# Moving splits, sums and raw weight loads in the last stage of an attention, expert and gated-layer kernel

## The chip, the cores and the metric

The kernel runs on one core of a Trainium2 chip. The metric is the device time of one launch in microseconds, as the median of several runs. Below, PE is the matrix engine (TensorE), DVE is VectorE, ACT is ScalarE, POOL is GpSimd and SP is SyncE, which here only issues DMAs.

## The reference

Three parts follow each other. The change is in the third; its core is quoted, the first two are told.

1. Attention without softmax: for each of 8 x 8 heads, `kv = k^T v`, `out = q kv`, then a root-mean-square norm of each row. This gives 4608 tokens of width 512.
2. A mixture of 8 experts: each token goes to the expert of its largest logit, through `relu(x w1) w2`, and is weighted by its softmax probability.
3. A gated layer over all 4608 tokens, width 512 to 1536 to 512:

```python
gate = 1.0 / (1.0 + np.exp(-(x @ w_gate)))
val = x @ w_val
return (gate * val @ w_out).astype(np.float32)
```

## The kernel before

The third part starts about 630 us into the span and is cut into 60 steps, 0 to 59. Tokens come in five blocks, `b` = 0 to 4 (`NB`); each block has 12 steps (`NJ`), one for each 128 of the 1536 inner columns. Step `s` is column slice `j = s % 12` of block `s // 12`. In blocks 1 to 4 a step holds two halves of 512 tokens.

Numbers are carried as pairs: each operand is split by ACT into a rounded high part (a copy) and by DVE into the low part (a subtraction), and each product is three matmuls, high by high, high by low, low by high. A split is therefore one ACT instruction followed by one DVE instruction.

**The gated unit.** `glu_unit` (matmuls in lines 1010 to 1012) computes gate and value of a step by Strassen's scheme in Winograd's form: seven products, numbered 1, 6, 7, 5, 2, 4, 3 in that order, of six 128x512 matmuls each. They go to the `gv` banks of PSUM, of which four rotate. DVE sums them (line 1014), ACT applies two sigmoids (1034, 1043), and DVE multiplies (1044, 1045) into two tiles `g` of the step.

**Spots.** Between the products the unit calls `at(p)`, and `prepare(s, p)` then issues other work. `SPOTS = (0, 1, 6, 7, 5, 2, 4, 3)` is their order in time: spot 0 before product 1, spot 1 after it, 6 after product 6, and so on, 3 at the step's end. Each engine executes what is issued to it in the order of issue, so the order in which `prepare` calls its parts is the order of each queue. This order is written out by hand.

**Inputs of the next block (Y).** During the last steps of a block the next block's rows are loaded (`load_y`), weighted (`weigh_y`), transposed on PE into a `gv` bank and copied to `yraw` by ACT (`flip_y`, line 1284), then summed (`sum_y`, line 1257) and split (`split_y`, ACT 1252, DVE 1253) into the seven right-hand operands. `YPLAN` gives the step and spot of each letter; splits and sums there are 1024 columns wide.

**Output products.** Blocks 0 and 1 multiply `g` by `w_out` plainly (`out_step`, lines 1380 to 1382, operands from `ready_o` and `load_o`). From block 2 (`FIRST` = 24) the output also goes by Strassen, in chunks. A chunk `(b, n, m)` is one of seven products `n` for one of six pairs `m` of column slices: 12 matmuls of 128x256 in `run_chunk` (lines 1480 to 1482). `place_chunks` puts products 1 and 7 of pair `m` into step 6 + m of the block itself, and products 2, 4, 6, 5, 3 into the first five steps after it, six chunks a step. For the last block these stand alone after step 59, at the end of the program. `ready_chunk` forms and splits a chunk's left operand (ACT 1453, DVE 1446; for n = 7 one more DVE subtraction first, for n = 2 one more after), `load_chunk` fetches its weights three chunks ahead, `sum_g` combines two pairs of `g` tiles by two DVE instructions (1463, 1464), and `combine` takes a finished product out of PSUM. `gh` and `gl`, the split operands, have three buffers each. `chunk_step` calls all of these at each spot from step 30 (`OPEN`); it stands last in `prepare`, behind the Y work.

**Combined output weights.** In steps 24 to 29 `sums_o` loads two raw rows of `w_out` (DMA, line 1398), subtracts quarters of them (four DVE instructions, 1403), splits both (ACT 1407, DVE 1408) and stores them (`wp_d`, 1409).

Of the kernel before, what the change touches and what calls it, by code (L numbers as in the profile page):

```python
# [25 lines left out]
NB = 5  # L26
# [58 lines left out]
def attention_moe_glu_kernel(  # L85
# [271 lines left out]
    with ExitStack() as st:  # L357
# [342 lines left out]
        for b in range(B):  # L700
# [6 lines left out]
            for r in range(5):  # L707
# [22 lines left out]
                early = b == B - 2  # L730
# [135 lines left out]
        for n in range(NFRONT * NJ1 + 1):  # L866
            t, j = divmod(n, NJ1)
# [343 lines left out]
    with ExitStack() as st:  # L1211
# [4 lines left out]
        NJ = F2 // 128  # L1216
# [106 lines left out]
        def new_wos():  # L1323
            return xp.tile([128, 2, DM], F32R, tag=wos_tags.pop(), name="wos")
# [43 lines left out]
        def out_step(*steps):  # L1368
            work = []
            for sz in steps:  # L1370
                if sz in step_at:
                    b, h, k = step_at[sz]
                    if k == 0:
                        acc[b, h] = [pac.tile([128, DM], F32, tag=f"ac{i}", name=f"ac{i}") for i in range(HT)]
                    work.append((b, h, k, split_o.pop(sz), *split_g.pop(sz)))
            for i in range(HT):
                for b, h, k, wos, gh, gl in work:
                    o, cs = acc[b, h][i], slice(i * 128, i * 128 + 128)
                    wh, wl = wos[:, 0], wos[:, 1]
                    nc.tensor.matmul(out=o, lhsT=gh[:, cs], rhs=wh, start=(k == 0), stop=False)  # L1380
                    nc.tensor.matmul(out=o, lhsT=gh[:, cs], rhs=wl, start=False, stop=False)  # L1381
                    nc.tensor.matmul(out=o, lhsT=gl[:, cs], rhs=wh, start=False, stop=(k == NJ - 1))  # L1382
                    if k == NJ - 1:
                        store_out(b, h, i, len(work) > 1)
# [3 lines left out]
        def sums_o(s, spot):  # L1388


            m = s - FIRST
            if not 0 <= m < NJ // 2:
                return
            if spot == 0:
                for i, pool in enumerate((y0p, late_pool[0])):
                    k = 2 * m + i
                    wo_raw[i] = pool.tile([128, DM], F32, tag="wo", name="wo", bufs=1)
                    nc.sync.dma_start(out=wo_raw[i], in_=w_d[k // 4][:, k % 4, 1024:1536])
            if spot == 5:
                b11, b12 = (wo_raw[0][:, n * 256:n * 256 + 256] for n in range(2))  # L1400
                b21, b22 = (wo_raw[1][:, n * 256:n * 256 + 256] for n in range(2))
                for o, x, y in ((b11, b12, b11), (b12, b22, b12), (b22, b22, b11), (b21, b21, b22)):
                    nc.vector.tensor_tensor(out=o, in0=x, in1=y, op=ALU.subtract)
            if spot in (2, 3):
                i = int(spot == 3)
                src, t = wo_raw[i], new_wos()
                nc.scalar.activation(out=t[:, 0], in_=src, func=ACTF.Copy)
                nc.vector.tensor_tensor(out=t[:, 1], in0=src, in1=t[:, 0], op=ALU.subtract)
                nc.sync.dma_start(out=wp_d[2 * m + i][:, :, :], in_=t.bitcast(F32))
# [6 lines left out]
        chunks, chunk_pos, chunks_ready, chunk_at, sum_at = [], [], [], {}, {}  # L1416

        def place_chunks(b):

            s0 = NJ * b  # L1420
            early = [(6, 5, 4), (7, 5, 4), (8, 5, 4), (9, 5, 4), (10, 5, 4), (11, 5, 4)]
            if b == NPLAIN:
                early[0:3] = [(7, 6, 5), (7, 2, 4), (8, 5, 4)]
            for m, (j, *spots) in enumerate(early):
                for spot, n in zip(spots, (1, 7)):
                    chunk_at.setdefault((s0 + j, spot), []).append((b, n, m))
                sum_at.setdefault((s0 + max(j + 1, 2 * m + 2), 1), []).append((b, m))
            seq = [(b, n, m) for m in range(6) for n in (2, 4)] + [(b, n, m) for n in (6, 5, 3) for m in range(6)]
            for i, c in enumerate(seq):
                chunk_at.setdefault((s0 + NJ + i // 6, SPOTS[1 + i % 6]), []).append(c)  # L1430

        def load_chunk(q):
            if q < len(chunks):
                b, n, m = chunks[q]
                src, odd, half = OPERAND[n]
                nc.sync.dma_start(out=b_slots[q % 4].bitcast(F32), in_=src[2 * m + odd][:, :, half * 256:half * 256 + 256])

        def ready_chunk(q):


            if q >= len(chunks):
                return
            b, n, m = chunks[q]
            g = G[b]
            a11, a12, a21, a22 = (2 * m, 0), (2 * m + 1, 0), (2 * m, 1), (2 * m + 1, 1)
            sub = lambda o, x, y: nc.vector.tensor_tensor(out=o, in0=x, in1=y, op=ALU.subtract)  # L1446
            if n == 7:
                src = free_g.pop(0)
                sub(src, g[a11], g[a21])
            else:  # L1450
                src = g[{1: a11, 2: a12, 4: a22, 6: a11, 5: a21, 3: a12}[n]]
            hi, lo = (ws.tile([128, HC], F32R, tag=t, name=t, bufs=3) for t in ("gh", "gl"))
            nc.scalar.activation(out=hi, in_=src, func=ACTF.Copy)  # L1453
            sub(lo, src, hi)
            split_c[q] = (hi, lo)
            if n == 2:
                sub(g[a12], g[a12], g[a11])
            elif n != 1:
                free_g.append(src)

        def sum_g(b, m):
            g = G[b]
            nc.vector.tensor_tensor(out=g[2 * m, 1], in0=g[2 * m, 1], in1=g[2 * m + 1, 1], op=ALU.add)
            nc.vector.tensor_tensor(out=g[2 * m, 0], in0=g[2 * m, 1], in1=g[2 * m, 0], op=ALU.subtract)
# [66 lines left out]
        b_slots, later_o = [], []  # L1531
# [20 lines left out]
                load_chunk(q)  # L1552

        def chunk_step(s, spot):
            for b, m in sum_at.get((s, spot), ()):
                sum_g(b, m)
            now = 8 * s + SPOTS.index(spot)
            if later_o:
                later_o.pop(0)()
            if now in chunk_pos:  # L1560
                q = chunk_pos.index(now)
                run_chunk(q)
                load_chunk(q + 3)
            q = len(chunks_ready)
            while q < len(chunks) and chunk_pos[q] <= now + 3 and (q < 2 or chunk_pos[q - 2] <= now):
                chunks_ready.append(q)
                ready_chunk(q)
                q += 1

        yr = {}  # L1570

# [65 lines left out]
        def prepare(s, spot):  # L1637


            b, j = divmod(s, NJ)  # L1640
            if spot == 0:
                load_wt(s + 1)
                if s + 2 <= NJ:
                    load_raw(s + 2, s + 1)
                load_rows(s + 2)
                decode_late(s)
                sum_w(s + 1)
            if spot == 6:
                ready_o(s, 1)
                load_o(s + 1, 0)  # L1650
                load_o(s + 1, 1)
            if spot == 1:
                group(s + 1, 0)
            if spot == 7:
                out_step((s, 0))
            if spot == 2:
                group(s + 1, 1)
            if spot == 4:
                ready_o(s + 1, 0)
                out_step((s, 1))  # L1660
            if b + 1 < NB:
                for what, do in TURNS[min(b, 1)].get((j, spot), ()):
                    what(b + 1, do)
                if s == 9 and spot == 0:
                    hold_y(mw[1].tile([128, 2, 2, 2, HC], F32R, tag="w2r1", name="w2r1"))
                if s == 11 and spot == 3:
                    hold_y(yA[0][:, 0:2])
                if b and j == NJ - 1 and spot:
                    free_y.append(Y.pop((b, spot)))
                for what in YPLAN[min(b, 1)].get((j, spot), ""):  # L1670
                    y_step(b + 1, what)
            if b > 1:
                for what in YPLAN[1].get((j + NJ, spot), ""):
                    y_step(b, what)
            if spot == 3:
                decode_late2(s)
            sums_o(s, spot)
            if (s, spot) == (FIRST, 0):
                yslots.extend(xp.tile([128, XW], F32, tag="xg", name="yr", bufs=4) for _ in range(2))
                free_g.extend(xp.tile([128, XW], F32, tag="xg", name="yr", bufs=4)[:, 0:HC] for _ in range(2))  # L1680
            if (s, spot) == (OPEN, 3):
                open_chunks()
            chunk_step(s, spot)

        bank = lambda n: pgv.tile([128, 512], F32, tag="gv", name="gv")
        tmp = lambda n: ws.tile([128, HC], F32, tag=n, name=n, bufs=1)
# [11 lines left out]
        OPEN = FIRST + 6  # L1698
# [43 lines left out]
```

## Time and profile before

| | |
|---|---|
| median of 3 runs | 1504.77 us (1502.82 to 1508.97) |
| the profiled execution | 1506.11 us, its span 1504.0 us |
| PE matmul / weight load busy | 1430.7 us (95%) / 1241.8 us (83%) |
| DVE, ACT, POOL busy | 1008.2 us (67%), 675.0 us (45%), 254.3 us (17%) |
| mean granted PE clock | 0.990 |
| HBM traffic | 250 GB/s over the span |

Busy is the time in which an engine executes; a waiting instruction is idle time. A clock of 1.00 is full speed. The shares are means over stages that differ, so the stretches that the change touches are read one by one below.

### The profile page before, as it was taken

How to read it: one execution, taken by the hardware profiler on the slowest of the kernel's cores; microseconds unless marked ns; L12 is line 12 of the kernel's file. 1: busy time of each engine (PE TensorE's matmuls, PEld its weight loads, DVE VectorE, ACT ScalarE, POOL GpSimd, SP SyncE). 2: the span in 40 equal slices, each digit the busy share in tenths (PEclk: the TensorE clock that was granted, in tenths of full speed). 3: DMA queues.
4: the chain of work that ended last, by engine and by line, in shares of the span. 5: the costliest groups of instructions: out<-in, count | busy, mean ns of one | idle time of the engine just before them, and what ended most of it. 6: DMA issues, size and time to landing. Idle time of an engine off the chain costs nothing.

```text
span 1504.0 us, 24818 instructions
## 1 busy us (share of the span) xinstructions
PE 1430.7 (95%) x9302; PEld 1241.8 (83%) x9302; DVE 1008.2 (67%) x1594; ACT 675.0 (45%) x1080; POOL 254.3 (17%) x350
## 2 busy tenths in 40 slices
PE   6988999999999999999999999999899999999995
PEld 6887789999999997778888777788788887998885
DVE  1667868888888886568766665456755567555663
ACT  3666455556556557555433332232433324322242
POOL 1021122322212222020111001020023200131014
PEclk9999999999999999999999999999999999999998
DMA  9977598998986758499976557785466654565544
GB/s 306 342 261 260 173 355 286 283 309 291 289 291 189 256 197 277 156 359 331 352 253 250 203 209 279 283 294 184 153 211 225 223 182 154 196 214 200 187 124 129
DMA packets 189707, 365.33 MB, mean 243 GB/s; under 512 B 22544, under 2 KB 114448, under 8 KB 182416
## 3 DMA queue, kind: packets, MB, share of 16 engines
q1 hardware_dynamic: 177408, 330.37, 65.0%
q0 software_dynamic: 10816, 32.08, 5.9%
q8 instruction: 75, 1.23, 0.3%
q10 hardware_dynamic: 1360, 1.26, 0.2%
q14 instruction: 48, 0.39, 0.1%
HBM read 301.31 MB, written 74.93 MB: 250 GB/s over the span
## 4 chain that ended last, share of the span: by engine, by line
PE 44%; DVE 6%; DMA 3%; ACT 2%; issue 1%; SPq 1%; POOL 0%; another core or an unknown queue 0%; POOLq 0%; DVEq 0%; ACTq 0%
PE gv L1010 8%; PE gv L1011 8%; PE gv L1012 8%; PE ac L1482 4%; PE ac L1480 3%; PE ac L1481 3%; DMA wo<-w_d 2%; PE ac L1380 2%; PE ac L1381 2%; PE ac L1382 2%; DVE u L1014 1%; PE gv L986 1%; PE gv L984 1%; PE gv L985 1%; PE tr L947 1%
## 5 line engine op out<-in xcount | busy, mean ns | idle before, releaser
L279 PE MATMUL ph<-xh,w1h 128*128 128x256 f32 x576 | 168.4, 292 | 5.6 <-ACT xh L261 4.6
L280 PE MATMUL ph<-xh,w1l 128*128 128x256 f32 x576 | 164.8, 286 | 0.9 <-DVE w1l L237 0.9
L281 PE MATMUL ph<-xl,w1h 128*128 128x256 f32 x576 | 164.9, 286 | 0.0
L1014 DVE TENSOR_TENSOR u<-u,gv 128x512 f32<-128x512 f32 x144 | 98.5, 684 | 95.9 <-PE gv L1012 90.8
L1482 PE MATMUL ac<-wos,gl 128*128 128x256 f32 x504 | 145.0, 288 | 9.8 <-DVE gl L1446 9.4
L1480 PE MATMUL ac<-wos,gh 128*128 128x256 f32 x504 | 144.0, 286 | 5.5 <-ACT gh L1453 5.3
L1481 PE MATMUL ac<-wos,gh 128*128 128x256 f32 x504 | 142.6, 283 | 0.0
L1011 PE MATMUL gv<-half,wt 128*128 128x512 f32 x336 | 131.7, 392 | 0.7 <-DVE half L1253 0.7
L1010 PE MATMUL gv<-half,wt 128*128 128x512 f32 x336 | 132.0, 393 | 0.0
L1012 PE MATMUL gv<-half,wt 128*128 128x512 f32 x336 | 130.9, 389 | 0.0
L279 PEld LDWEIGHTS ph<-xh,w1h 128*128 128x128 f32 x576 | 112.1, 195 | 8.0 <-ACT xh L261 4.8
L280 PEld LDWEIGHTS ph<-xh,w1l 128*128 128x128 f32 x576 | 112.2, 195 | 2.8 <-DVE w1l L237 1.1
L281 PEld LDWEIGHTS ph<-xl,w1h 128*128 128x128 f32 x576 | 112.0, 194 | 0.3 <-DVE xl L263 0.3
L1482 PEld LDWEIGHTS ac<-wos,gl 128*128 128x128 f32 x504 | 96.2, 191 | 14.1 <-DVE gl L1446 13.4
L336 PE MATMUL py<-w2l,hh 128*128 128x512 f32 x272 | 106.8, 393 | 0.1
L335 PE MATMUL py<-w2h,hh 128*128 128x512 f32 x272 | 106.7, 392 | 0.0
L337 PE MATMUL py<-w2h,hl 128*128 128x512 f32 x272 | 106.1, 390 | 0.0
L1480 PEld LDWEIGHTS ac<-wos,gh 128*128 128x128 f32 x504 | 96.2, 191 | 11.9 <-ACT gh L1453 7.6
L1043 ACT ACTIVATE u<-u 128x512 f32<-128x512 f32 x48 | 30.4, 633 | 153.0 <-DVE u L1014 150.7
L1481 PEld LDWEIGHTS ac<-wos,gh 128*128 128x128 f32 x504 | 96.3, 191 | 3.1
L1490 POOL DMA_INDIRECT out_dram<-ot,to x48 | 52.8, 1101 | 272.0 <-ACT ot L1512 180.4
L349 POOL DMA_INDIRECT y_d<-y,sidx x36 | 40.9, 1135 | 286.0 <-ACT y L345 96.5
(370 smaller groups left out, 3668.4 us busy)
## 6 DMA issues: line engine op xcount, KB each, us to landing
wt<-wt_d SPq DMA_DIRECT2D x36, 1536.0 KB
half<-in_moe_w_dram SPq DMA_DIRECT2D x96, 512.0 KB
w1r<-in_moe_w_dram SPq DMA_DIRECT2D x40, 512.0 KB
w2r<-in_moe_w_dram SPq DMA_DIRECT2D x40, 512.0 KB
wos<-wp_d SPq DMA_DIRECT2D x72, 256.0 KB
wos<-wo_d SPq DMA_DIRECT2D x54, 256.0 KB
rows<-w_d SPq DMA_DIRECT2D x24, 512.0 KB
wt<-wt_d SPq DMA_DIRECT2D x48, 256.0 KB
```

Source lines behind the costliest of these rows:

```text
L279: nc.tensor.matmul(out=o, lhsT=bh[:, c, cs], rhs=hi[:, c, 0:n], start=(c == 0), stop=False)
L280: nc.tensor.matmul(out=o, lhsT=bl[:, c, cs], rhs=hi[:, c, 0:n], start=False, stop=False)
L281: nc.tensor.matmul(out=o, lhsT=bh[:, c, cs], rhs=lo[:, c, 0:n], start=False, stop=(c == KC - 1))
L335: nc.tensor.matmul(out=o, lhsT=hi[:, f, cs], rhs=bh[:, f, :], start=first, stop=False)
L336: nc.tensor.matmul(out=o, lhsT=hi[:, f, cs], rhs=bl[:, f, :], start=False, stop=False)
L1010: nc.tensor.matmul(out=o, lhsT=wh, rhs=yh[:, c, :], start=first and c == 0, stop=False, skip_group_check=True)
L1011: nc.tensor.matmul(out=o, lhsT=wh, rhs=yl[:, c, :], start=False, stop=False, skip_group_check=True)
L1012: nc.tensor.matmul(out=o, lhsT=wl, rhs=yh[:, c, :], start=False, stop=last and c == 1, skip_group_check=True)
L1014: add = lambda out, a, c: nc.vector.tensor_tensor(out=out, in0=a, in1=c, op=ALU.add)
L1480: nc.tensor.matmul(out=o, lhsT=gh[:, cs], rhs=wh, start=fresh and i % 2 == 0, stop=False, skip_group_check=True)
L1481: nc.tensor.matmul(out=o, lhsT=gh[:, cs], rhs=wl, start=False, stop=False, skip_group_check=True)
L1482: nc.tensor.matmul(out=o, lhsT=gl[:, cs], rhs=wh, start=False, stop=stop, skip_group_check=True)
```

## The change

Five things move; no arithmetic is added or taken away.

- `sums_o`: the two raw loads for pair `m` are issued at spot 3 of the step before instead of spot 0 of the step; the subtractions at spot 7 instead of 5; the two splits and stores at spots 5 and 2 instead of 2 and 3.
- Product 1 of the early chunks runs at spot 2 instead of 5.
- `chunk_step` is called ahead of the Y work in `prepare`, and within it the chunk runs and is readied before the pending output sums and before `sum_g`; a chunk is readied up to 4 spots ahead instead of 3.
- `sum_g` of pairs 3 to 5 of blocks 2 and 3 moves to the second step after the block (spots 1, 5 and 4).
- The extra subtraction that stood with product 2 stands with product 6 in blocks 2 and 3.

```diff
             m = s - FIRST
-            if not 0 <= m < NJ // 2:
-                return
-            if spot == 0:
+            if spot == 3 and -1 <= m < NJ // 2 - 1:
+                m += 1
                 for i, pool in enumerate((y0p, late_pool[0])):
...
+                return
+            if not 0 <= m < NJ // 2:
+                return
-            if spot == 5:
+            if spot == 7:
...
-            if spot in (2, 3):
-                i = int(spot == 3)
+            if spot in (5, 2):
+                i = int(spot == 2)
...
-            early = [(6, 5, 4), (7, 5, 4), (8, 5, 4), (9, 5, 4), (10, 5, 4), (11, 5, 4)]
+            early = [(6, 2, 4), (7, 2, 4), (8, 2, 4), (9, 2, 4), (10, 2, 4), (11, 2, 4)]
             if b == NPLAIN:
-                early[0:3] = [(7, 6, 5), (7, 2, 4), (8, 5, 4)]
+                early[0:3] = [(7, 6, 5), (7, 2, 4), (8, 2, 4)]
...
-                sum_at.setdefault((s0 + max(j + 1, 2 * m + 2), 1), []).append((b, m))
+                sum_at.setdefault((s0 + max(j + 1, 2 * m + 2), 1) if m < 3 or b == NB - 1 else (s0 + NJ + 1, (1, 5, 4)[m - 3]), []).append((b, m))
...
-            if n == 2:
+            if n == (2 if b == NB - 1 else 6):
                 sub(g[a12], g[a12], g[a11])
-            elif n != 1:
+            if n not in (1, 2):
                 free_g.append(src)
...
         def chunk_step(s, spot):
-            for b, m in sum_at.get((s, spot), ()):
-                sum_g(b, m)
             now = 8 * s + SPOTS.index(spot)
-            if later_o:
-                later_o.pop(0)()
             if now in chunk_pos:
...
-            while q < len(chunks) and chunk_pos[q] <= now + 3 and (q < 2 or chunk_pos[q - 2] <= now):
+            while q < len(chunks) and chunk_pos[q] <= now + 4 and (q < 2 or chunk_pos[q - 2] <= now):
...
+            if later_o:
+                later_o.pop(0)()
+            for b, m in sum_at.get((s, spot), ()):
+                sum_g(b, m)
...
+            if s > OPEN:
+                chunk_step(s, spot)
             if b + 1 < NB:
                 for what, do in TURNS[min(b, 1)].get((j, spot), ()):
...
                 open_chunks()
-            chunk_step(s, spot)
+                chunk_step(s, spot)
```

## Rows read from the trace of the kernel before

**Rows 1.** Windows of the third part: busy us (count) by engine, PE clock, DMA share, GB/s
```profile
918.00:989.00 71.00, 64.86 (x288) 52.00 (x287) 36.52 (x65) 21.08 (x39) 5.23 (x8) 1.00 0.74 275
989.00:1045.00 56.00, 56.00 (x299) 47.70 (x298) 32.57 (x51) 19.04 (x33) 9.23 (x14) 1.00 0.68 236
1045.00:1092.00 47.00, 41.35 (x227) 34.53 (x225) 37.66 (x51) 18.18 (x30) 0.00 (x0) 1.00 0.45 160
1233.00:1280.00 47.00, 42.34 (x224) 35.60 (x223) 37.60 (x51) 18.71 (x30) 0.00 (x0) 0.96 0.45 158
```

**Rows 2.** PE's waits, 918 to 989 us: total us, times, longest
```profile
PE gv L1010 <- ACT yraw L1284: 6.1, 4, 1.9
```

**Rows 3.** PE's waits, 1045 to 1092 us
```profile
PE ac L1482 <- DVE gl L1446: 3.8, 6, 1.2
PE ac L1480 <- ACT gh L1453: 1.8, 2, 1.3
```

**Rows 4.** PE's waits on DVE, 1233 to 1280 us
```profile
PE ac L1482 <- DVE gl L1446: 2.8, 4, 1.2
```

**Rows 5.** PE's waits, 1438 to 1492 us
```profile
PE ac L1482 <- DVE gl L1446: 2.8, 6, 0.8
PE ac L1480 <- ACT gh L1453: 1.7, 2, 1.1
```

**Rows 6.** The chain that ended last, whole span, shares by line
```profile
PE gv L1010 8%; PE gv L1011 8%; PE gv L1012 8%; PE ac L1482 4%; PE ac L1480 3%; PE ac L1481 3%; DMA wo<-w_d 2%; PE ac L1380 2%; PE ac L1381 2%; PE ac L1382 2%; DVE u L1014 1%; PE gv L986 1%; PE gv L984 1%; PE gv L985 1%; PE tr L947 1%
```

**Rows 7.** Waits of ACT and DVE, 918 to 989 us
```profile
ACT wos L1407 <- DVE wo L1403: 23.4, 4, 6.2
...
DVE wo L1403 <- DMA wo<-w_d: 27.5, 8, 6.9
```

**Rows 8.** Timeline around step 27's start: start, us, engine, line, [idle before, releaser]
```profile
932.42 0.39 PE L1012 MATMUL gv<-half,wt 128*128 128x512 f32 x1
...
933.81 0.58 ACT L1284 ACTIVATE yraw<-tr 128x512 f32<-128x512 f32 x1
...
934.44 0.50 PE L1010 MATMUL gv<-w2r,wt 128*128 128x512 f32 x1 [1.64 <-ACT yraw L1284]
...
934.78 0.40 PE L1011 MATMUL gv<-w2r,wt 128*128 128x512 f32 x1
...
935.01 0.40 PE L1012 MATMUL gv<-w2r,wt 128*128 128x512 f32 x1
```

**Rows 9.** Timeline of SP's DMA queue, 936 to 942 us
```profile
938.54 1.21 SPq L1294 DMA_DIRECT2D wt<-wt_d  x2
...
940.34 1.21 SPq L1398 DMA_DIRECT2D wo<-w_d  x2
```

**Rows 10.** The chain from 918 to 989 us, in order of time: its longest DMA
```profile
940.82 8.78 DMA wo<-w_d
```

**Rows 11.** Timeline of step 34: DVE's queue, and PE's matmuls of one chunk
```profile
1045.20 1.23 DVE L1253 TENSOR_TENSOR w1r<-yraw,w1r 128x1024 fp32r<-128x1024 f32 x1 [0.26 <-ACT w1r L1252]
...
1046.46 1.23 DVE L1257 TENSOR_TENSOR yraw<-yraw 128x1024 f32<-128x1024 f32 x1
...
1047.60 0.68 DVE L1463 TENSOR_TENSOR gm<-gm,gm 128x512 f32<-128x512 f32 x1
...
1048.04 0.28 PE L1480 MATMUL ac<-wos,gh 128*128 128x256 f32 x1
...
1048.15 0.28 PE L1481 MATMUL ac<-wos,gh 128*128 128x256 f32 x1
...
1048.93 0.69 DVE L1446 TENSOR_TENSOR gl<-rows,gh 128x512 fp32r<-128x512 f32 x1
...
1049.67 0.39 PE L1482 MATMUL ac<-wos,gl 128*128 128x256 f32 x1 [1.24 <-DVE gl L1446]
```

**Rows 12.** Timeline of DVE after the last step, at product 6's end
```profile
1469.53 1.40 DVE L1505 TENSOR_TENSOR wos<-wos,ac 128x512 f32<-128x512 f32 x2 [3.20 <-PE ac L1482]
1470.84 0.69 DVE L1446 TENSOR_TENSOR gl<-gm,gh 128x512 fp32r<-128x512 f32 x1
```

## The prediction

> **What bounds the kernel now.** I read the windows of the third part first. From 989 to 1045 us PE is busy for all 56.00 us: there the kernel goes at PE's own pace and no reordering of other engines can gain. The change touches stretches where PE is not full: 918 to 989 (64.86 of 71.00), 1045 to 1092 (41.35 of 47.00) and 1233 to 1280 (42.34 of 47.00) [rows 1]; after step 59 there is a fourth. So I went on to PE's waits there, because only what PE waits for can shorten this part. They name three releasers. In 918 to 989 it is ACT's copy of the transposed inputs, 6.1 us in 4 waits [rows 2]. In the next two stretches and after step 59 it is the split of a chunk's left operand, `gh` by ACT and `gl` by DVE: 3.8 + 1.8 = 5.6 us in 8 waits [rows 3]; 2.8 us in 4 waits on `gl` [rows 4] and the same 1.8 us in 2 on `gh`, so 4.6 in 6; 2.8 + 1.7 = 4.5 us in 8 [rows 5].
>
> The chain of waits comes last, and the reader should see why it is not the sum. It gives the DMA of raw weights 2% of the span, about 30 us [rows 6]. But in that stretch PE idles only 6.1 us [rows 2]: while the chain runs through the DMA, PE still works. A stall on the chain is worth what PE lost by it.
>
> What one wait costs PE: matmuls of 512 columns start 0.23 us apart (934.78 to 935.01); with the wait of 1.64 us the steps were 932.42 to 934.44 and 934.44 to 934.78, that is 2.02 + 0.34 - 0.46 = 1.90 [rows 8]. So each wait costs its idle time plus 0.26 us of restart.
>
> **Raw weight loads a step sooner.** The cause of the 6.1 us: the two loads stand on SP behind the next gated weights (issued at 938.54; the raw loads at 940.34 [rows 9]) and land 7.9 to 9.1 us after their issue (8.78 in the row, one of four [rows 10]). DVE's subtractions wait for them, 27.5 us in 8 waits, and ACT's split waits for the subtractions, 23.4 us in 4 [rows 7]. Both queues are in order, so the copy out of the transpose's bank, 0.58 us of work at 933.81, comes that late, and product 6 of the next step starts 0.05 us after it ends [rows 8]. After the change the 12 loads (two in each of six steps) are issued at spot 3 of the step before, ahead of the gated weights on SP, and the subtractions come four spots into the step. That is at least product 1, 6 and 7 later, 18 x 0.23 = 4.1 us, and with the weights no longer ahead of them I expect them landed. The four waits go: 6.1 + 4 x 0.26 = 7.1 us. The four subtractions at spot 7 and the splits at 5 and 2 are the same instructions as before and lie beside `out_step` matmuls; DVE is busy 36.52 of 71.00 us there [rows 1], so they cost nothing; without that cover six times four subtractions and two splits would fall on PE at once. The loads move past SP's gated weights and the y row; those have a whole step, (42 + 24) x 0.23 = 15.2 us of PE or more. The stores move forward with the splits.
>
> **Chunks ahead of Y.** Step 34 shows the pattern. DVE has a Y split (1045.20), a Y sum (1046.46, 1.23 us), then `sum_g` (two instructions, 1047.60 to 1048.93) and only then the `gl` of the chunk that PE began at 1048.04; PE stood 1.24 us [rows 11]. After the change `gl` stands ahead of the sum and of `sum_g`, and the chunk itself one product later, 6 x 0.23 = 1.4 us. In that order `gl` is done some 2.5 us earlier (1.23 + 1.33) against a wait of 1.24, so this wait goes.
>
> Step 35 is the heaviest and decides whether the waits come back elsewhere. Its PE time is seven products and two chunks: 42 x 0.23 + 24 x 0.12 = 12.5 us (0.11 to 0.12 between starts of 256 columns [rows 11]). DVE before: seven sums and products, one chunk subtraction and four `gl` at about 0.62 (half of the 1.33 plus short gaps give 0.60 to 0.67), three Y splits and one Y sum at about 1.2 (1.26 between 1045.20 and 1046.46), `sum_g` 1.33 and the extra subtraction of product 2 at 0.62: 12 x 0.62 + 4 x 1.2 + 1.33 + 0.62 = 14.2 us, more than PE has. After: 12.2 us, just under it. The wait was an overload of DVE by 1.7 us in this step, and more after it; what goes from steps 34 to 36 is three `sum_g` and three extra subtractions, 3 x 1.33 + 3 x 0.62 = 5.9 us, about the 5.6 us that PE waited [rows 3]. They come back in steps 37 and 38, where six chunks a step give PE 42 x 0.23 + 72 x 0.12 = 18.3 us against 12 to 15 us of DVE, and the windows of such steps show no wait. So both stretches lose their waits: 5.6 + 8 x 0.26 = 7.7 us and 4.6 + 6 x 0.26 = 6.2 us. In the second the granted clock was 0.96 over 47.00 us [rows 1]: part of it ran at the lower level, 1.2 GHz, after the waits, which is 0.04 x 47 = 1.9 us more. Sum 7.7 + 6.2 + 1.9 = 15.8 us. The bounds: nothing, if DVE's backlog merely moves; all 15.8. I take 14.8, leaving 1 us for waits that stay in step 35, as 12.2 us of DVE in 12.5 is nearly full.
>
> The Y work now comes behind one chunk split per spot, 0.62 us. Its users are a step or several products later, and three Y operands are needed in step 36 itself: the last, `h`, is split two chunks and two products before product 4, 2 x 1.44 + 2 x 1.4 = 5.7 us, for a sum, ACT's split and DVE's (3.5 us). The flips stand behind the chunk at spot 4 instead of ahead of it; the copy must then be done within products 3 and 1, 2.8 us, and takes 0.58 [rows 8].
>
> **After step 59.** Thirty chunks follow without other PE work. Three things are gained. The first two splits are ahead of the last step's sums instead of behind them, 1.5 us. At the end of product 6 the `gl` of the next chunk stood behind two additions out of PSUM (1469.53, 1.40 us, then `gl` at 1470.84 [rows 12]); now it is ready before. That saves the 0.80 us wait and its restart there, of which I keep 0.6, since the third one behind is then late; the same place at the end of product 5 saves 1.1 us. Sum 3.2 of 4.5 + 8 x 0.26 = 6.6 us [rows 5]; `sum_g` of pair 5 and the additions out of PSUM stay. Bounds 0 and 6.6.
>
> **The sum.** 7.1 + 14.8 + 3.2 = 25.1 us. No matmul, byte or instruction is added. The profiled execution took 1506.11 us (span 1504.0), 1.3 above the median of 1504.77; 1506.1 - 25.1 = 1481.0, and against the median 1479.7. I say 1480.
>
> **A rule weighed.** Four like waits on the transpose's copy look like a shortage of banks [rows 2]; in 989 to 1045 us steps with transposes and the same four banks show none [rows 1]. The Trainium skill, "Perfetto Trace Analysis", Optimization Strategy, says of such consistent bubbles that there may not be enough SBUF or PSUM for the next tile; by it the 7.1 us would stay, which is the second rival below.
>
> **The rivals.**
> 1. DVE's backlog moves instead of going: the Y splits, now behind the chunks, become what PE waits for in steps 35 and 36. For it: 12.2 of 12.5 us. Against: 5.9 us leave these steps. Half of 15.8 then stays and the tail gains 1.5: 7.1 + 7.9 + 1.5 = 16.5, so 1488. Chance 0.18.
> 2. The four banks hold the transposes' product back whatever ACT does: 7.1 us stay, 1487. Against: the copy ran 0.58 us at 933.81, just after the queue came free [rows 8]. Chance 0.07.
> 3. The change does nothing there: loads and splits come early but wait for buffers (three `gh`, one raw tile for each row), and each wait is found again. 1501 to 1506, say 1503. Chance 0.05.
> 4. Slower: SP. A raw load waits for the last split of its step to have read the tile, and the gated weights stand behind it on SP. In the trace the weights were issued at 938.54, and the raw loads behind them landed at 949.6 [rows 9, 10]; so the weights take at most 11 us. If SP were held some 5 us more, to 9 us into a step, they would come after the next step's first product. With 4.5 us more in each of six steps: 27 us, against 18.0 from chunks and tail, and the 7.1 not gained: 1514. Against it: the last split is now two products ahead of the step's end. Chance 0.04.
> 5. The chain is right and the whole 30 us of the DMA come back beside the 18: 1457. Against: PE's waits [rows 2]. Chance 0.01.
>
> The forecast has 0.65. Its own range is 1476 (all 15.8 and most of the 6.6) to 1485 (5 us left). For 8 in 10 with the first two rivals: 1474 to 1494. Measurement tells 0.5%, 7.5 us, from no change: faster than 1497.2 with 0.65 + 0.18 + 0.07 + 0.01 = 0.91, within 0.05, slower 0.04.
>
> **What would show it.** In the profile after: no wait of PE on `yraw`, and no idle DVE or ACT on `wo`, in steps 25 to 30; no `gl` or `gh` wait of over 0.5 us in steps 34 to 36 and 46 to 48; PE full there as in 989 to 1045; after step 59 some 3 us of waits left, at the ends of products 2, 6 and 5. Wrong would be new waits of PE on Y operands (lines 1252, 1253), on gated weights, or on `sum_g` in steps 37, 38, 49 and 50.

## The result, and the profile after

The changed kernel took 1482.93 us (1481.51 to 1484.19, 4 runs) against 1503.8 (1499.09 to 1508.97, 4 runs) of the kernel before: ratio 0.986, interval 0.9826 to 0.9895. The forecast was 1480. The profiled execution after has a span of 1482.1 us, 21.9 less than before.

The windows of about the same stretches, here cut at the steps (columns as in [rows 1]; steps 26 to 29, steps 30 to 33, steps 34 to 36, and steps 46 to 48):

```profile
917.40:979.20 61.80, 61.80 (x281) 51.12 (x281) 35.05 (x62) 20.47 (x37) 5.71 (x9) 1.00 0.86 319
979.20:1037.70 58.50, 57.53 (x305) 49.34 (x304) 32.95 (x51) 18.10 (x32) 9.70 (x14) 1.00 0.63 221
1037.70:1082.80 45.10, 43.77 (x248) 38.16 (x247) 35.12 (x46) 20.36 (x32) 0.00 (x0) 1.00 0.53 181
1219.00:1264.10 45.10, 43.77 (x247) 38.14 (x246) 35.13 (x46) 20.36 (x32) 0.00 (x0) 1.00 0.54 181
```

PE is full in the first, which before it was not [rows 1]. In the last two it still loses 1.3 us each, and the clock of the last is back at 1.00. In the second, where PE was full before [rows 1], it now loses 1.0 us: step 32 takes 14.14 us instead of 13.11. PE's waits, in 1010 to 1083, 1219 to 1265 and after step 59, in that order:

```profile
PE gv L1010 <- DVE u L1014: 2.3, 3, 1.0
...
PE gv L1010 <- DVE u L1014: 1.3, 2, 0.9
...
PE ac L1484 <- DVE gl L1448: 1.8, 2, 1.0
```

The copy of the transpose is gone as a releaser [rows 2], and so is every wait on a chunk's `gh` or `gl` in steps 34 to 36 and 46 to 48 [rows 3, 4]. In their place stands a wait that the trace of before does not have: a product of the gated unit waits for DVE's sums `u`. After step 59 a part of the waits is left [rows 5]. (Lines 1480 to 1482, 1446 and 1453 of before are 1482 to 1484, 1448 and 1455 now.)

Stretches are compared better by PE's own order than by windows. PE executes the same matmuls in each step in both kernels, so the start of a step can be found by counting matmuls back from the last one; the gated unit alone has 42 in each. Length of each step in us from these starts (sums over the steps; "end" is all after step 59):

```
steps      before   after    saved
24, 25      32.62   32.76   -0.14
26 to 30    84.90   77.22    7.68
31 to 36    93.54   88.12    5.42
37 to 41    84.74   84.66    0.08
42 to 48   103.80   96.66    7.14
49 to 59   157.28  157.28    0.00
end         64.20   60.72    3.48
sum        621.08  597.42   23.66
before 24  882.92  884.68   -1.76
```

So the third part saved 23.7 us; the forecast's terms for the same stretches were 7.1, 14.8 (both chunk stretches) and 3.2. The time before step 24 was 1.8 us longer in this profile, though the kernels differ there only by the two loads at step 23's end. Over the 14 profiles of this study it lay between 881.9 and 886.7 us. Medians of whole runs carry this spread; step lengths from step 25 on mostly repeat to some hundredths (the changed kernel profiled again: 77.21, 88.12, 96.62). The experiments below are therefore read by steps, and the medians stand beside them.

### The profile page after: what moved, and what is told of

It is laid out like the page before. It is cut to its first block, busy times and chain, and to the rows that moved or that the text cites. A ratio compares the mean times of both kernels' runs of the same rounds, so it can differ in the third digit from the quotient of the medians.

```text
span 1482.1 us, 24848 instructions
## 1 busy us (share of the span) xinstructions
PE 1424.9 (96%) x9302; PEld 1244.6 (84%) x9302; DVE 1008.5 (68%) x1594; ACT 677.9 (46%) x1080; POOL 257.5 (17%) x350
## 3 DMA queue, kind: packets, MB, share of 16 engines
q8 instruction: 75, 1.23, 0.3%
## 4 chain that ended last, share of the span: by engine, by line
PE 50%; DVE 4%; ACT 1%; DMA 1%; issue 1%; POOL 0%; SPq 0%; POOLq 0%; ACTq 0%; DVEq 0%
PE gv L1010 9%; PE gv L1011 9%; PE gv L1012 9%; PE ac L1484 4%; PE ac L1483 4%; PE ac L1482 4%; PE ac L1380 2%; PE ac L1382 2%; PE ac L1381 2%; PE gv L986 1%; PE gv L984 1%; PE gv L985 1%; DVE u L1014 1%; PE tr L947 1%; DMA rows<-w_d 1%; DVE gl L1448 1%
## 5 line engine op out<-in xcount | busy, mean ns | idle before, releaser
L1492 POOL DMA_INDIRECT out_dram<-ot,to x48 | 56.8, 1184 | 258.7 <-ACT ot L1514 172.6
```

## Experiments

**1. The raw weights alone.** The kernel before, with the whole change to `sums_o` and nothing else:

```diff
-            if spot == 0:
+            if spot == 3 and -1 <= m < NJ // 2 - 1:
...
-            if spot == 5:
+            if spot == 7:
...
-            if spot in (2, 3):
+            if spot in (5, 2):
```

> The kernel before, with the change to the raw weights alone (loads at spot 3 of the step before, subtractions at 7, splits at 5 and 2). Theory (the four waits on the transpose's copy are ACT held behind a split that waits for a late DMA): steps 26 to 30 shorten by 7.7 us together, as in the changed kernel, every other step keeps its length; about 1496. Rival (the four banks hold the product back): steps 26 to 30 keep their length when chunks are left alone; about 1504.

1497.18 us median, ratio 0.9965 (0.995 to 0.9979). Steps 26 to 30 took 77.21 us, 7.69 saved; steps 31 to 36 and 42 to 48 stayed (93.62 and 104.07). The banks are the same four, so a shortage of banks is not the cause; the second rival falls.

**2. The rest alone.** The changed kernel with `sums_o` as before (the diff above, backwards).

> The changed kernel with the raw weights as before. Theory (the two parts are independent): steps 26 to 30 keep the length of before, steps 31 to 36, 42 to 48 and the stretch after step 59 save 5.4, 7.1 and 3.5 us as in the changed kernel; about 1488 to 1490. Rival (part of the chunk gain comes from the earlier stretch ending sooner and leaving DVE or DMA ahead): under 12 us saved there.

1489.85 us, ratio 0.9912 (0.9886 to 0.9938). Saved: 5.57, 7.16 and 3.37 us in steps 31 to 36, 42 to 48 and at the end, as in the changed kernel. Steps 26 to 30 took 85.68: one of them was 21.4 us long, the others 15.4 to 17.3. The two parts are independent.

**3. Only the loads earlier.** The changed kernel, subtractions and splits back at spots 5, 2 and 3:

```diff
-            if spot == 7:
+            if spot == 5:
...
-            if spot in (5, 2):
-                i = int(spot == 2)
+            if spot in (2, 3):
+                i = int(spot == 3)
```

> The changed kernel, with the raw loads at spot 3 of the step before but subtractions and splits at spots 5, 2 and 3 as before. Theory (the wait was for the late landing, nothing else): steps 26 to 30 save the whole 7.7 us. Rival (the splits' places keep ACT free for the copy): under 4 us saved there, with waits on the transpose's copy left.

In the code the subtractions and splits also stand ahead of the loads, so that at spot 3 the old row is split before the next one is loaded. Steps 26 to 30: 77.22 us, 7.68 saved (1484.2 us median). The loads alone do it.

**4. Only the splits moved.** The changed kernel with the loads back at spot 0:

```diff
-            if spot == 3 and -1 <= m < NJ // 2 - 1:
-                m += 1
+            if not 0 <= m < NJ // 2:
+                return
+            if spot == 0:
...
-                return
-            if not 0 <= m < NJ // 2:
-                return
```

> The changed kernel, with the raw loads at spot 0 of the step as before, subtractions at 7 and splits at 5 and 2 as changed. Theory (late landing): the loads still land 8 to 9 us after their issue, some 11 us into a step; ACT and DVE wait for them as long as before or longer, and steps 26 to 30 save under 4 us. Rival (the splits' places count): 6 us or more saved there.

Steps 26 to 30 saved 6.22 us, but step 25 grew from 14.96 to 17.22, so 3.9 us in steps 24 to 30 (1485.07 us median). In 918 to 981 us DVE still waited for the loads, and PE had its one long wait in step 25 (899 to 940 us) on a sum behind them:

```profile
DVE wo L1403 <- DMA wo<-w_d: 20.0, 8, 4.5
```
```profile
PE gv L1010 <- DVE yr L1014: 1.8, 1, 1.8
```

Step 26, at 16.89 us, had no wait, but a granted clock of 0.91. The expectation named the landing as the only cause, and for steps 27 to 30, at 15.44 to 15.46 us, it missed; the rival's 6 us or more were saved in steps 26 to 30, though only 3.9 with steps 24 and 25. The reason is on SP. Its queue, around the start of step 28 of this kernel (949.38 us), and the store in step 27 of the kernel before (starting 931.27 us; the weights and raw loads behind it are in [rows 9], 7.3 and 9.1 us into the step):

```profile
947.23 2.23 SPq L1409 DMA_DIRECT2D wp_d<-wos  x2
949.56 1.21 SPq L1294 DMA_DIRECT2D wt<-wt_d  x2
...
951.35 0.90 SPq L1398 DMA_DIRECT2D wo<-w_d  x2
```
```profile
938.12 0.32 SPq L1409 DMA_DIRECT2D wp_d<-wos  x1
```

With the stores of the split weights done at the step's end, SP issues the next weights 0.2 us and the raw loads 2.0 us into the step. In the kernel before, the late split made a late store, the store stood on SP ahead of the next step's loads, and so the lateness passed on from step to step: the weights were issued 3.5, 6.5 and 7.3 us into steps 25, 26 and 27.

**5. Chunks behind the Y work again.** The changed kernel with `chunk_step` last in `prepare`, as before:

```diff
-            if s > OPEN:
-                chunk_step(s, spot)
...
-                chunk_step(s, spot)
+            chunk_step(s, spot)
```

> The changed kernel, with chunk_step back behind the Y work in each spot; sums and extra subtractions stay a step later. Theory (DVE was overloaded in steps 34 to 36 and 46 to 48, and moving 5.9 us of sums out is what counts): most of the saving there stays, at least 9 of the 12.4 us of these steps, about 1483 to 1486. Rival (the order is what counts: a split behind a Y sum and split is late by itself): over half comes back, 1490 or more.

1483.31 us, ratio 0.9877 (0.9857 to 0.9897). Saved 5.36, 7.05 and 3.88 us; the changed kernel saves 5.42, 7.14 and 3.48. So whether `chunk_step` stands ahead of the Y work or behind it is worth nothing that shows. The order inside `chunk_step` stays changed here, and no run undid it by itself. PE's waits of this kernel, 990 to 1265 us, are the same ones on `u`:

```profile
PE gv L1010 <- DVE u L1014: 4.1, 5, 1.0
```

**6. Sums back in place.** The changed kernel with `sum_g` and the extra subtraction as before:

```diff
-sum_at.setdefault((s0 + max(j + 1, 2 * m + 2), 1) if m < 3 or b == NB - 1 else (s0 + NJ + 1, (1, 5, 4)[m - 3]), []).append((b, m))
+sum_at.setdefault((s0 + max(j + 1, 2 * m + 2), 1), []).append((b, m))
...
-            if n == (2 if b == NB - 1 else 6):
+            if n == 2:
```

> The changed kernel, with all sum_g and the extra subtractions of product 2 back in their steps; order, spots and lookahead as changed. Theory (moving DVE's load out of steps 34 to 36 and 46 to 48 is what counts): these steps, 12.4 us shorter than before in the changed kernel, give back 6 us or more of it, about 1489 or later. Rival (the chunk's later place and the longer lookahead alone give the splits time enough): they give back under 2.5 us.

1489.61 us, ratio 0.9903 (0.9867 to 0.9939). Saved only 1.43 and 2.87 us in steps 31 to 36 and 42 to 48: 8.3 of 12.6 us came back. The waits (1010 to 1083, then 1219 to 1265 us) are not on `gl` but again on `u`, and longer:

```profile
PE gv L1010 <- DVE u L1014: 4.6, 3, 1.9
...
PE gv L1010 <- DVE u L1014: 3.6, 2, 1.9
```

A part of the 8.3 us is the clock: steps 35 and 47 ran at 0.89, and PE was busy for 14.2 us in each instead of 12.7. So DVE's load in these steps is what counted most; with the load back, its lateness shows at another of its results, the one that the new order puts late. The sums back together with experiment 8's later split were not run, so how much the load costs without that wait is open.

**7. Product 1 back at spot 5.** `early` as before (for block 2 too), all else changed:

```diff
-            early = [(6, 2, 4), (7, 2, 4), (8, 2, 4), (9, 2, 4), (10, 2, 4), (11, 2, 4)]
+            early = [(6, 5, 4), (7, 5, 4), (8, 5, 4), (9, 5, 4), (10, 5, 4), (11, 5, 4)]
```

> The changed kernel, with product 1 of the early chunks back at spot 5 (so it is readied at spot 0, with the lookahead of 4). Theory (what counts is DVE's load, and u3 behind the split of product 7): within 1.5 us of the changed kernel in steps 31 to 48, and the waits on u in steps 32, 34, 35 stay. Rival (the later place is what removes the waits on gl of product 1): waits on gl of 0.5 us and more come back in steps 34, 35, 46, 47, 2.5 us or more in all.

1482.11 us median. Saved 6.06, 7.22 and 3.34 us: 0.7 more in steps 31 to 48 than the changed kernel, so the later place of product 1 gains nothing.

**8. Product 7 readied a spot later.** The changed kernel, lookahead 3 for product 7 alone:

```diff
-            while q < len(chunks) and chunk_pos[q] <= now + 4 and (q < 2 or chunk_pos[q - 2] <= now):
+            while q < len(chunks) and chunk_pos[q] <= now + (3 if chunks[q][1] == 7 else 4) and (q < 2 or chunk_pos[q - 2] <= now):
```

> The changed kernel, with the left operand of product 7 readied at most 3 spots ahead, others 4; so its subtraction and split stand behind the sum u3 (spot 7) instead of ahead of it (spot 6). Theory: the new waits of PE on DVE's u in steps 32, 34, 35, 46 and 47 (0.97, 0.40, 0.94, 0.39, 0.93 us) are product 4 waiting for u3, which stands behind that split; they go, 3.6 us plus 0.2 each of restart: 4 to 4.6 us less than the changed kernel, about 1478.5. Rival (DVE is simply full in these steps): the waits move to gh or gl of product 7 or 2, and the time stays within 1 us of the changed kernel.

1477.87 us, ratio 0.9842 (0.9824 to 0.986). Steps 31 to 36 took 85.37 us and steps 42 to 48 95.24, 2.75 and 1.42 less than the changed kernel: 4.17 us, as the theory said. Step 35 in the changed kernel shows why (DVE and ACT in the order of time, and PE's two lines around the wait; 1014 is a sum of the unit, 1448 the subtraction and the split for product 7, 1257 a Y sum):

```profile
1055.64 0.68 DVE L1014 TENSOR_TENSOR u<-u,gv 128x512 f32<-128x512 f32 x1
...
1056.24 0.68 DVE L1448 TENSOR_TENSOR rows<-gm,gm 128x512 f32<-128x512 f32 x1
...
1057.02 0.63 ACT L1455 ACTIVATE gh<-rows 128x512 fp32r<-128x512 f32 x1 [2.55 <-DVE rows L1448]
...
1057.68 0.69 DVE L1448 TENSOR_TENSOR gl<-rows,gh 128x512 fp32r<-128x512 f32 x1 [0.76 <-ACT gh L1455]
...
1058.30 1.22 DVE L1257 TENSOR_TENSOR yraw<-yraw 128x1024 f32<-128x1024 f32 x1
...
1058.95 0.28 PE L1484 MATMUL ac<-wos,gl 128*128 128x256 f32 x1
...
1059.43 0.68 DVE L1014 TENSOR_TENSOR u<-u,gv 128x512 f32<-128x512 f32 x1
...
1060.17 0.50 PE L1010 MATMUL gv<-w2r,wt 128*128 128x512 f32 x1 [0.94 <-DVE u L1014]
```

Product 4 adds into the bank that holds product 7 of the unit. It may start only when DVE has read that bank for `u3` (1059.43). DVE comes to it 3.2 us after the chunk's subtraction at 1056.24, because it also stands idle 0.76 us for ACT's part of the split. With the split a spot later, the same place reads:

```profile
1055.40 1.22 DVE L1257 TENSOR_TENSOR yraw<-yraw 128x1024 f32<-128x1024 f32 x1
...
1056.53 0.68 DVE L1014 TENSOR_TENSOR u<-u,gv 128x512 f32<-128x512 f32 x1
...
1057.13 0.68 DVE L1448 TENSOR_TENSOR rows<-gm,gm 128x512 f32<-128x512 f32 x1
...
1058.11 0.28 PE L1484 MATMUL ac<-wos,gl 128*128 128x256 f32 x1
...
1058.23 0.40 PE L1010 MATMUL gv<-w2r,wt 128*128 128x512 f32 x1
```

`u3` (1056.53) is ahead, and product 4 follows the chunk with no wait. DVE has the same work in both kernels; only the place of product 7's subtraction and split differs.

**9. Three spots ahead for all chunks.** `now + 3` in that line, as before the change; timed beside experiments 10 to 12.

> The changed kernel with the lookahead of 3 for all chunks. Theory: in steps 31 to 48 like the version with product 7 late (within 1 us); after step 59 the splits stand behind the last step's sums and behind the additions at the ends of products 6 and 5 again, and 2.5 to 3.5 us come back there. Rival (what helps after step 59 is the order within a spot): under 1 us comes back there.

1480.18 us, ratio 0.9851 (0.9834 to 0.9869). Steps 31 to 36 and 42 to 48: 85.47 and 95.33 us, as with product 7 alone. The end took 63.37 us against 60.19 of the changed kernel beside it: 3.2 us given back of the 4.0 gained there. PE's waits after step 59:

```profile
PE ac L1484 <- DVE gl L1448: 2.8, 6, 0.8
PE ac L1482 <- ACT gh L1455: 1.1, 1, 1.1
```

These are nearly the waits of before [rows 5]: after step 59 the longer lookahead is most of the gain, and what else moved gives at most the other 0.8 us.

**10. The changed kernel again.**

> The changed kernel itself, timed beside the next three: 1482 to 1484; PE's step lengths from step 24 on as in its first profile, within 0.1 us a step; the time before step 24 differs by some us from profile to profile.

1480.92 us, ratio 0.9855 (0.9835 to 0.9874). The median lies 1.1 us below the expected range. Steps as in its first profile; the end 60.19 us instead of 60.72.

**11. Product 7 late, again** (the kernel of experiment 8).

> The version with product 7 readied 3 spots ahead, beside the changed kernel: 4 to 4.6 us less than it (theory: u3 ahead of that split), rival 1 us or less.

1480.23 us, ratio 0.9835 (0.9815 to 0.9855). By steps 85.45 and 95.24 us, 4.05 less than the changed kernel in the same two stretches. By the median only 0.7 less, and the two ratios' intervals overlap; its profile had the latest start of step 24 of all, 886.73 us against 883.46. The 4 us are shown by the steps, not by these runs.

**12. And the last block's last sum a step later.** The kernel of experiment 8, with

```diff
-(s0 + max(j + 1, 2 * m + 2), 1) if m < 3 or b == NB - 1 else (s0 + NJ + 1, (1, 5, 4)[m - 3])
+(s0 + NJ + 1, (1, 5, 4)[m - 3]) if m > 2 and b < NB - 1 else (s0 + max(j + 1, 2 * m + 2) + (b == NB - 1 and m == 5), 1)
```

> That version, with the last block's last sum_g a step later (step 61, spot 1, instead of 60). Theory: after step 59 the wait of 0.96 us on gl in the second step is sum_g's two instructions ahead of that split; it goes, 1.1 us less there. Rival: DVE is full there, and the wait comes back at the next split; under 0.4 us.

1476.63 us, ratio 0.9825 (0.9806 to 0.9844): the lowest median of all, though its interval overlaps that of experiment 11. The end took 58.93 us, 1.25 less than in experiment 11, while steps 49 to 59 took 0.25 more, so 1.0 us by steps. PE's waits after step 59, one long one fewer:

```profile
PE ac L1484 <- DVE gl L1448: 1.1, 2, 0.9
```

## Why the prediction was right, and where it was not

- **Raw loads: right in size, its cause incomplete.** 7.1 us forecast, 7.7 measured, and the loads alone give it. DVE's waits for them fell from 27.5 us [rows 7] to 1.6. New are the two things that experiment 4 shows: SP's stores passed the lateness on, and moving the splits alone removes the loss in steps 27 to 30 and saves 3.9 us over steps 24 to 30. The loads now stand ahead of the weights on SP:

```profile
932.99 1.26 SPq L1397 DMA_DIRECT2D wo<-w_d  x2
934.35 0.91 SPq L1294 DMA_DIRECT2D wt<-wt_d  x2
```

- **"They cost nothing": right, though the engines wait.** ACT and DVE still stand in 917 to 995 us, now for PE: a split waits for a tile that `out_step` reads. The prediction did not see these waits; they cost PE nothing, as the full window shows.

```profile
DVE wos L1410 <- ACT wos L1409: 24.0, 5, 4.8
ACT wos L1409 <- PE ac L1382: 22.5, 7, 3.8
```

- **Chunks: forecast 14.8, measured 12.6.** The count of DVE's work in step 35, 14.2 us against PE's 12.5, was the right reason for most of it: DVE was busy for 41.0 us in steps 34 to 36 before and for 35.1 after, as forecast, and with the sums back 8.3 of the 12.6 us are lost again (experiment 6). But DVE was not full in these 51.4 us: its results come late also because it stands idle for ACT's part of a split, as in step 35 above. The part about order, "`gl` is done some 2.5 us earlier (1.23 + 1.33)", gave too much to the 1.23 of the Y sum: with `chunk_step` behind the Y work again all but 0.15 us of the 12.6 stay (experiment 5).
- **The clock's 1.9 us are not an addition.** Before, steps 34 to 36 (clock 1.00 [rows 1]) took 51.39 us and steps 46 to 48 (0.96) 51.38. In experiment 1, with these chunks as before, steps 46 to 48 ran at 1.00 and took 51.65: PE, no longer slowed, waited for `gl` and `gh` as in the first stretch, 5.6 us instead of 4.6. So the lower clock lengthened nothing there; it took the place of waits.
- **The term that came out too large** is "I take 14.8, leaving 1 us for waits that stay in step 35". It looked at the Y work and the flips that come behind a split, not at the unit's own sums. The longer lookahead also brought product 7's subtraction and split from spot 7 to spot 6, ahead of `u3`, and product 4 waits for `u3`. That cost 4.1 us in five steps (experiments 8 and 11), of which the 1 us left covered a part. It is the wait that takes the place of the one removed, and in step 32 it is one where none had been; the first rival had named the Y splits for it, which never held PE in steps 34 to 36. Without it the chunk stretches save 16.7 us, more than the forecast's bound of 15.8, since steps 32, 33 and 42 to 45, which it did not count, are then 0.2 us shorter each. What shortened those was not tried.
- **After step 59: 3.2 forecast, 3.5 measured**, by the lookahead, as experiment 9 shows. What was left at `sum_g` was there too, and experiment 12 removes 1.25 us of it.
- **The rivals.** DVE's backlog: in part, at another place. The banks: fallen (experiment 1). "Nothing changes" and SP: no trace of either; SP issues the weights 1.4 us behind the raw loads. The chain's 30 us: the chain of 917 to 980 us is now all PE, and what came was PE's 7.7 us.
- **The sum.** 25.1 forecast, 23.7 by steps. That it is so near is in part luck: the other terms came out 0.6 and 0.3 us above their forecasts and hid some of the 2.2 that the chunks fell short. The medians differ by 20.9; the 1.8 us before step 24 in the two profiles show how much of such a difference the unchanged part can make.

## What to carry to other kernels

Size a reordering by what the bounding engine waits for in the stretch, not by the chain's share: here the chain held 2% in one DMA, and PE had lost 7.7 us to it. When work is issued earlier on an in-order queue, list every result that is now behind it, above all reads of a bank into which the next product accumulates. Where a feeding engine has more work in a step than the bounding one, move work out of the step, and then check the order of what stays: here one split ahead of `u3` cost 4.1 us, and with the same work and that split a spot later the wait was gone.

## What was not expected of the hardware

Identical work before step 24 ended between 881.9 and 886.7 us in 14 profiles, a spread of 4.8 us, while step lengths in the last part mostly repeated to some hundredths. The spread is there early: PE's matmul number 2001 started between 167.2 and 174.1 us. What makes it was not tried.

A lower granted clock cost time in one place and none in another. In step 26 of experiment 4, without a wait, a clock of 0.91 took 16.89 us where step 27 took 15.44. In steps 46 to 48 of the kernel before, where PE waited for DVE, a clock of 0.96 went with 51.38 us, and in experiment 1 a clock of 1.00 with 51.65.
